# Local attention keys cut into chunks of 96, 96 and 64, twice over

## The chip, the cores and the metric

The kernel runs on one core of a Trainium2 chip. The metric is the device time in microseconds (us). The kernel before takes 934.98 us, the median of three runs (934.98 to 938.12). A core has five engines that work side by side and wait for each other by semaphores: TensorE (PE in the profile; its weight loads are PEld), VectorE (DVE), ScalarE (ACT), GpSimd (POOL) and SyncE (SP), which here only issues DMAs.

## The reference

For 8 batches and 8 heads there are 512 local and 32 global positions of 64 numbers each. A local query attends to the 32 global keys and to the local keys at a distance of at most 32; a global query attends to all 544 keys. The result goes through a feed-forward layer with a softplus in its middle, over 4608 tokens of 512 numbers.

```python
k_all = concat([k_g, k_l]); v_all = concat([v_g, v_l])
out_g = sm(scale * q_g @ k_all.T) @ v_all
s_ll  = where(abs(i - j) <= 32, scale * q_l @ k_l.T, -1e9)
out_l = sm(concat([scale * q_l @ k_g.T, s_ll])) @ concat([v_g, v_l])
x = concat([out_g, out_l]) as [B * S, H * D]
h = x @ w_in                                   # 512 -> 2048
g = maximum(h, 0) + log1p(exp(-abs(h)))
return g @ w_out                               # 2048 -> 512
```

`sm` subtracts the row's maximum, takes exp and divides by the sum plus 1e-9.

## The kernel before

**Tiles.** Two heads make a pair, so there are 32 pairs, four to a batch. The first four pairs (batch 0) go through a scheme of their own in the opening. Each of the other 28 has its local keys cut into six chunks of up to 96, and each chunk stands behind the 32 global keys on the 128 output rows of a score product. The queries are the columns. The 1024 score columns of a head go to two PSUM banks of 512, p = 0 and p = 1. A table `PARTS` says which query columns meet which chunk: 160, 192, 160 columns in the first bank and 32, 192, 192, 96 in the second, that is 7 products a head, 14 a pair (the two heads of a pair work on the two halves of the array's rows). The value products turn chunks back into queries: 8 a head, 16 a pair.

**Softmax without a product.** The maximum over keys of a query lies on partitions, so a transposing reduce (L384, L446) gives maxima or sums of 32 by 32 blocks into a small tile (`mt` for maxima, `zt` for sums), `spread` (L395, POOL) lays its four parts side by side, `gather` (L397 to L405, five small `tensor_reduce` on DVE) folds the blocks that belong to one query or to the global queries, `maxima` copies the answer to the four quadrants of partitions (L410), `lift` (L417) transposes it into a tile of columns that `probs` subtracts on POOL (L429, L431), and `exps` (L435) runs on ACT. For the sums `sums_rest` runs `gather`, four reciprocals (L458) and a transpose (L460). `values_out` multiplies two PSUM banks by that on DVE (L482, 384 and 224 columns), and POOL adds up the global part (L484).

**Feed-forward.** `split_x` (L566 to L579) cuts the attention's result x into a rounded part `xh` (L578, ACT) and the rest `xl` (L579; DVE for the third and fourth pair of a batch, POOL for the others). For every 128 of the 2048 inner features TensorE computes h from xh and xl (12 products of 512 columns), then ACT, DVE (L659) and POOL make `gh` and `gl`, and TensorE computes o from these (12 products).

**Order.** Two lists of step codes set the order of the work on every engine: `OPENING`, and `STEADY`, which runs six times (blocks 1 to 6, four pairs each). S is scores, M maxima, P probs, E exps, Z sums_first, R sums_rest, V values, X and x are split_x of a pair, and h, g, o are a feature block's first half, second half and output. `inorder` chains each engine's instructions in that order. A block ends with "... o R2 E31 h Z3 g X0 X1 R3 o o o V2" and the next starts with "x2 x3 o h g h g": V2 computes the values of two pairs, x2 and x3 split them, and the h that follows opens the next batch. Two shorter lists, `LAST` and `GLOBAL`, close the kernel with feed-forward work alone. PSUM is full: the two `h` banks are shared by the feed-forward's h, by half of a pair's scores and by one of the two value tiles of V2, so the h that follows V2 needs the DVE multiplications that empty that value tile.

**Loads.** For each pair SP loads raw queries and keys (`load`, 736 and 704 columns) and the value chunks.

Of the kernel before, what the change touches and what calls it, by code (L numbers as in the profile page):

```python
# [8 lines left out]
F32 = mybir.dt.float32  # L9
# [12 lines left out]
LOW = -3.0e38  # L22
KW = 96
NPC = 2
QW = (352, 320)
RW = (736, 704)
EW = (0, 736)
FIRST = (0, 9)
PARTS = (((0, 0, 0, 160), (1, 64, 160, 192), (2, 192, 352, 160)),
         ((2, 64, 0, 32), (3, 0, 32, 192), (4, 128, 224, 192), (5, 224, 416, 96)))  # L30
# [33 lines left out]
GW = 76  # L64
# [19 lines left out]
def moe_over_global_local_attention(  # L84
# [57 lines left out]
    def key_masks():  # L142
        near = mask[:, 1]
        nc.vector.memset(near, 0.0)
        for o, w, x0, rows in ((224, 160, 0, P), (32, 64, 0, P), (128, 96, 64, P), (416, 64, 0, 64)):
            r = near[0:rows, o:o + w]
            pool0(nc.gpsimd.affine_select(r, r, pattern=[[1, w]], compare_op=ALU.is_ge, fill=NEG, base=32 + x0, channel_multiplier=-1))
            pool0(nc.gpsimd.affine_select(r, r, pattern=[[-1, w]], compare_op=ALU.is_ge, fill=NEG, base=32 - x0, channel_multiplier=1))
        nc.vector.memset(near[0:32], 0.0)
        for o in (0, 32, 96, 192, 224, 352, 384, 416):  # L150
            nc.vector.memset(near[0:32, o:o + 32], NEG)
        nc.vector.memset(near[64:128, 416:512], NEG)
        for o, w, at in ((256, 160, 0), (32, 192, 160), (224, 160, 352)):
            nc.vector.tensor_copy(mask[:, 0, at:at + w], near[:, o:o + w])
# [167 lines left out]
    def load(m, p):  # L322
        raw = pl.tile([P, rows_of(736)], F32, tag="raw", name=f"raw{m}_{p}", bufs=3)
        order["load"] = after(nc.sync.dma_start(out=raw[:, :RW[p]], in_=qk[m - M0, :, EW[p]:EW[p] + RW[p]]), "load").ins
        st["raw", m, p] = raw
# [6 lines left out]
    def scores(m, p, onv):  # L332
# [26 lines left out]
        inorder(nc.vector.tensor_reduce(windows(mt, 4 + 16 * p, 36, 2, 16), s.rearrange("p h (b k) -> p h b k", k=32),  # L359
# [3 lines left out]
    def scores_all(m):  # L363
# [33 lines left out]
    def gather(mt, op):  # L397
        e0 = 4 * GW + 1
        for u, off in ((-1, 2), (2, 3)):
            inorder(nc.vector.tensor_reduce(grid(mt, e0 + u, (7, 6), (1, 2)), grid(mt, 4 + u - 2 * (u < 0), (12, 6), (1, 2), (off, 2), (GW, 4)), axis=AX.XY, op=op))  # L400
        inorder(nc.vector.tensor_reduce(grid(mt, e0 + 1, (7, 6), (4, 2)), grid(mt, 4 + 1, (12, 6), (7, 2), (GW, 4)), axis=AX.X, op=op))
        g = e0 + 42
        inorder(nc.vector.tensor_reduce(grid(mt, g, (1, 2)), grid(mt, 4 + 4, (36, 2), (12, 3), (3, 2), (GW, 4)), axis=AX.XYZ, op=op))
        inorder(nc.vector.tensor_reduce(grid(mt, e0 + 4, (21, 2), (7, 3)), mt[0:32, g:g + 2].unsqueeze(2).unsqueeze(3).to_broadcast([32, 2, 3, 1]), axis=AX.X, op=op))
        return mt[:, e0:e0 + 42]  # L405

    def maxima(m):
        e = gather(st.pop(("mt", m)), ALU.max)
        for a in range(1, 4):
            inorder(nc.vector.tensor_reduce(e[32 * a:32 * a + 32, 0:40], e[0:32, 0:40].unsqueeze(2), axis=AX.X, op=ALU.max))  # L410
        st["e", m] = e

    def lift(m, p):
        e = st["e", m]
        k = QW[p] // 32
        mb = st["mb", m, p] = pl.tile([P, 2, 352], F32, tag="mb", name=f"mb{m}_{p}", bufs=2)
        inorder(nc.vector.transpose(mb[:, :, :QW[p]].rearrange("p h (s k) -> p h s k", k=32),  # L417
                            windows(e, FIRST[p], 21, 2, k).unsqueeze(3).to_broadcast([P, 2, k, 32])))

    def probs(m, p, engine):  # L420
# [6 lines left out]
        for so, sd, mo, md, w in (((0, 352, 0, 192, 160),), ((32, 192, 0, 128, 192),))[p]:  # L427
            sw = pairs(s, 512, so, sd, w)
            inorder(engine.tensor_tensor(sw, sw, pairs(mb, 352, mo, md, w), op=ALU.subtract))  # L429
        for so, mo, w in (((160, 64, 192),), ((0, 64, 32), (416, 224, 96)))[p]:  # L430
            inorder(engine.tensor_tensor(s[:, :, so:so + w], s[:, :, so:so + w], mb[:, :, mo:mo + w], op=ALU.subtract))  # L431
# [7 lines left out]
    SEG = ((lambda t: t[:, 0:128].unsqueeze(1), 0, 1, 128), (lambda t: windows(t, 160, 224, 2, 192), 128, 2, 192))  # L439

    def sums_first(m):
        zt = pl.tile([P, rows_of(349 + 40)], F32, tag="mt", name=f"zt{m}", bufs=3)
        inorder(nc.gpsimd.memset(zt[0:32, 349:389], 1e-9))
        inorder(nc.gpsimd.memset(windows(zt, 0, 36, 3, 4), 0.0))
        for p in range(NPC):
            inorder(nc.vector.tensor_reduce(windows(zt, 4 + 16 * p, 36, 2, 16), st["s", m, p].rearrange("p h (b k) -> p h b k", k=32),  # L446
# [4 lines left out]
    def sums_rest(m):  # L451
        z0 = gather(st["zt", m], ALU.add)[0:32, 0:40]
        z = st.pop(("zt", m))[:, 0:40]
        inorder(nc.vector.tensor_reduce(z[0:32], bass.AP(z0.tensor, z0.offset, [list(z0.ap[0]), [1, 40], [44, 2]]), axis=AX.X, op=ALU.add))
        zr = pl.tile([P, ROW], F32, tag="zr", name=f"zr{m}", bufs=2)
        for a in range(4):
            h = a // 2
            inorder(nc.vector.reciprocal(zr[32 * a:32 * a + 32, 0:19], z[0:32, 21 * h:21 * h + 19]))  # L458
        rb = st["rb", m] = pl.tile([P, rows_of(608)], F32, tag="rb", name=f"rb{m}", bufs=2)[:, 0:608]
        inorder(nc.vector.transpose(rb.rearrange("p (s k) -> p s k", k=32), zr[:, 0:19].unsqueeze(2).to_broadcast([P, 19, 32])))  # L460

    def values(m, ps):
# [12 lines left out]
    def values_out(m):
# [4 lines left out]
        y = xa[b, j] = pl.tile([P, 608], F32, tag="xa", name=f"xa{b}_{j}", bufs=4)  # L480
# [83 lines left out]
    def split_x(b, j):  # L564
# [263 lines left out]
```

## Time and profile before

| what | value |
|---|---|
| median of 3 runs | 934.98 us (934.98 to 938.12) |
| the profiled execution | 936.42 us, of which span 934.6 us |
| mean granted TensorE clock | 0.998 |
| PE busy | 920.9 us, 99% |
| PE weight loads | 761.8 us, 82% |
| DVE busy | 578.8 us, 62% |
| ACT busy | 496.3 us, 53% |
| POOL busy | 445.8 us, 48% |
| instructions | 14703 |

The span reaches from the first to the last instruction on the core; the execution's own time has about 1.8 us around it. PE's busy time is drawn with modelled ends, so the starts of neighbouring PE rows tell more than their durations. A row such as "x4" is a run of like instructions, and its second column is the time from the first one's start to the last one's end. In brackets stands how long the engine was idle before and what ended the idle time.

### The profile page before, as it was taken

How to read it: one execution, taken by the hardware profiler on the slowest of the kernel's cores; microseconds unless marked ns; L12 is line 12 of the kernel's file. 1: busy time of each engine (PE TensorE's matmuls, PEld its weight loads, DVE VectorE, ACT ScalarE, POOL GpSimd, SP SyncE). 2: the span in 40 equal slices, each digit the busy share in tenths (PEclk: the TensorE clock that was granted, in tenths of full speed). 3: DMA queues.
4: the chain of work that ended last, by engine and by line, in shares of the span. 5: the costliest groups of instructions: out<-in, count | busy, mean ns of one | idle time of the engine just before them, and what ended most of it. 6: DMA issues, size and time to landing. Idle time of an engine off the chain costs nothing.

```text
span 934.6 us, 14703 instructions
## 1 busy us (share of the span) xinstructions
PE 920.9 (99%) x5472; PEld 761.8 (82%) x5472; DVE 578.8 (62%) x1173; ACT 496.3 (53%) x834; POOL 445.8 (48%) x666
## 2 busy tenths in 40 slices
PE   8899999999999999999999999999999999999997
PEld 5778788888888888888888888888888888888896
DVE  5789987576665766567666766567666766311211
ACT  5767777554464535453564636463564626544453
POOL 3344668454554635463654545363644545322221
PEclk9999999999999999999999999999999999999999
DMA  9535431302022030302022030302022020200000
GB/s 354 201 130 192 140 117 64 105 23 77 23 75 67 4 95 5 129 16 83 17 74 72 1 100 1 128 17 83 16 74 70 1 67 1 69 1 1 24 23 23
DMA packets 30696, 64.59 MB, mean 69 GB/s; under 512 B 7328, under 2 KB 7840, under 8 KB 30624
## 3 DMA queue, kind: packets, MB, share of 16 engines
q1 hardware_dynamic: 29888, 63.32, 20.3%
q8 instruction: 43, 0.70, 0.3%
q10 hardware_dynamic: 736, 0.33, 0.2%
q14 instruction: 29, 0.24, 0.1%
HBM read 54.20 MB, written 9.44 MB: 68 GB/s over the span
## 4 chain that ended last, share of the span: by engine, by line
PE 95%; DVE 2%; ACT 2%; issue 0%; ACTq 0%
PE o L157 41%; PE h L157 39%; PE s_ps L157 7%; PE v_ps L157 6%; ACT e L210 1%; PE s L157 1%; PE t L157 1%; DVE sums L207 0%; PE t0g L157 0%; PE dummy L157 0%; PE o0g L157 0%; PE s0g L157 0%; DVE p_1gl L258 0%; DVE wbitswo L610 0%; DVE mb L417 0%
## 5 line engine op out<-in xcount | busy, mean ns | idle before, releaser
L157 PE MATMUL o<-wo,gh 128*128 128x512 f32 x1088 | 340.5, 394 | 0.0
L157 PE MATMUL h<-xh,wi 128*128 128x512 f32 (+1 forms) x1152 | 339.5, 378 | 0.8 <-ACT yg L317 0.8
L663 POOL TENSOR_TENSOR gl<-e,gh 128x512 fp32r<-128x512 f32 x136 | 175.4, 1290 | 310.6 <-ACT gh L662 194.7
L659 DVE SCALAR_TENSOR_TENSOR e<-h,e 128x512 f32<-128x512 f32 x136 | 93.3, 686 | 249.7 <-ACT e L658 242.9
L157 PEld LDWEIGHTS h<-xh,wi 128*128 128x128 f32 x1152 | 212.1, 188 | 41.9 <-ACT yg L317 1.0
L157 PEld LDWEIGHTS o<-wo,gh 128*128 128x128 f32 x1088 | 200.6, 188 | 43.8 <-DVE wo L617 0.2
L157 PE MATMUL h<-xl,wi 128*128 128x512 f32 (+1 forms) x576 | 217.5, 378 | 0.0
L157 PE MATMUL o<-wo,gl 128*128 128x512 f32 x544 | 211.8, 389 | 0.0
L656 ACT ACTIVATE e<-h 128x512 f32<-128x512 f32 x136 | 81.1, 596 | 213.8 <-PE h L157 205.0
L662 ACT CAST gh<-e 128x512 fp32r<-128x512 f32 x136 | 84.4, 621 | 128.5 <-DVE e L659 128.5
L157 PEld LDWEIGHTS h<-xl,wi 128*128 128x128 f32 x576 | 108.4, 188 | 20.8 <-DVE xl L579 0.5
L157 PEld LDWEIGHTS o<-wo,gl 128*128 128x128 f32 x544 | 102.1, 188 | 21.8
L429 POOL TENSOR_TENSOR s<-s,mb 128x640 f32<-128x640 f32 (+1 forms) x55 | 93.9, 1708 | 16.1 <-DVE mb L417 9.6
L658 ACT ACTIVATE e<-e,one 128x512 f32<-128x512 f32 x136 | 98.5, 724 | 4.4
L657 ACT ACTIVATE e<-e 128x512 f32<-128x512 f32 x136 | 86.0, 632 | 4.3
L446 DVE TRANSPOSE_TENSOR_REDUCE zt<-s 128x32 f32<-128x1024 f32 x56 | 67.2, 1222 | 14.9 <-ACT s L435 14.9
L435 ACT ACTIVATE s<-s 128x1024 f32<-128x1024 f32 x56 | 58.5, 1056 | 30.0 <-POOL mt L377 17.0
L157 PE MATMUL s_ps<-raw 64*128 64x192 f32 (+2 forms) x672 | 61.9, 318 | 0.0
L395 POOL COPY mt<-mt 32x76 f32<-32x76 f32 x84 | 20.1, 239 | 83.5 <-DVE mt L384 72.2
L157 PEld LDWEIGHTS s_ps<-raw 64*128 64x128 f32 x672 | 51.9, 187 | 9.8 <-issue 9.6
L384 DVE TRANSPOSE_TENSOR_REDUCE mt<-s 128x32 f32<-128x1024 f32 x48 | 56.6, 1218 | 0.0
L157 PEld LDWEIGHTS v_ps<-s,v 128*64 128x64 f32 x896 | 49.0, 137 | 7.7 <-issue 4.9
(156 smaller groups left out, 845.0 us busy)
## 6 DMA issues: line engine op xcount, KB each, us to landing
raw<-in_qk SPq DMA_DIRECT2D x32, 352.0 KB, 3.0
v<-in_v SPq DMA_DIRECT2D x28, 384.0 KB, 3.3
raw<-in_qk SPq DMA_DIRECT2D x28, 368.0 KB, 3.9
wiraw<-in_w_in SPq DMA_DIRECT2D x16, 512.0 KB, 8.3
woraw<-in_w_out SPq DMA_DIRECT2D x16, 512.0 KB, 6.4
out<-ot SPq DMA_DIRECT2D x32, 256.0 KB, 2.1
v<-in_v SPq DMA_DIRECT2D x4, 512.0 KB, 9.0
raw<-in_qk SPq DMA_DIRECT2D x4, 416.0 KB, 8.6
```

Source lines behind the costliest of these rows:

```text
L157: order["pe"] = after(nc.tensor.matmul(*a, **k), "pe").ins
L384: inorder(nc.vector.tensor_reduce(windows(mt, 4 + 16 * p, 36, 2, 16), st["s", m, p].rearrange("p h (b k) -> p h b k", k=32), axis=AX.X, op ...
L395: inorder(nc.gpsimd.tensor_copy(mt[0:32, GW * a:GW * a + GW], mt[32 * a:32 * a + 32, 0:GW]))
L429: inorder(engine.tensor_tensor(sw, sw, pairs(mb, 352, mo, md, w), op=ALU.subtract))
L435: inorder(nc.scalar.activation(s, s, AF.Exp, scale=0.125))
L446: inorder(nc.vector.tensor_reduce(windows(zt, 4 + 16 * p, 36, 2, 16), st["s", m, p].rearrange("p h (b k) -> p h b k", k=32), axis=AX.X, op ...
L656: inorder(nc.scalar.activation(e, ph, AF.Abs))
L657: inorder(nc.scalar.activation(e, e, AF.Exp, scale=-1.0))
L658: inorder(nc.scalar.activation(e, e, AF.Ln, bias=one))
L659: inorder(nc.vector.scalar_tensor_tensor(e, ph, 0.0, e, op0=ALU.max, op1=ALU.add))
L662: inorder(nc.scalar.copy(gh, e))
L663: inorder(nc.gpsimd.tensor_tensor(gl, e, gh.bitcast(F32), op=ALU.subtract))
```

## The change

A head's local keys are cut into chunks of 96, 96, 64, 64, 96 and 96 (`KEYS`), and its queries start at column 0 and at 224 (`QUERIES`). Both banks then have the same parts, 160, 192 and 160 columns against three chunks of their own, and the same 1024 columns as before: 6 score products a head instead of 7 (12 a pair), 7 value products instead of 8 (14 a pair). What follows from it:

- `gather` has eight `tensor_reduce` instead of five, since the blocks of a query lie in other places; the small tiles have no guard columns any more, so POOL's memsets of them (L350, L377, L444) go. Maxima, sums and reciprocals have 44, 44 and 22 columns for 40, 40 and 19.
- `lift` makes 704 columns for both banks (704 and 640 before), the transpose of the reciprocals 704 for 608.
- `probs` of the second bank is two subtractions for three.
- `values_out` multiplies 352 and 288 columns. POOL's two additions are one of 2 x 32 columns and one of 32.
- `split_x` reads pieces of 2 x 128 and 2 x 160 columns, which overlap (576 columns for 512), where it read 128 and 2 x 192. Both ACT copies come first and then both subtractions; before it was copy, subtraction, copy, subtraction.
- The second load of a pair has 736 columns for 704, and `key_masks` builds the masks with 2 POOL selects for 8 and more DVE copies and memsets.

```diff
-PARTS = (((0, 0, 0, 160), (1, 64, 160, 192), (2, 192, 352, 160)),
-         ((2, 64, 0, 32), (3, 0, 32, 192), (4, 128, 224, 192), (5, 224, 416, 96)))
+KEYS = ((0, 96), (96, 96), (192, 64), (256, 64), (320, 96), (416, 96))
+QUERIES = (0, 224)
+PARTS = ((0, 0, 160), (64, 160, 192), (192, 352, 160))
...
     def gather(mt, op):
-        e0 = 4 * GW + 1
-        for u, off in ((-1, 2), (2, 3)):
-            inorder(nc.vector.tensor_reduce(grid(mt, e0 + u, (7, 6), (1, 2)), grid(mt, 4 + u - 2 * (u < 0), (12, 6), (1, 2), (off, 2), (GW, 4)), axis=AX.XY, op=op))
-        inorder(nc.vector.tensor_reduce(grid(mt, e0 + 1, (7, 6), (4, 2)), grid(mt, 4 + 1, (12, 6), (7, 2), (GW, 4)), axis=AX.X, op=op))
-        g = e0 + 42
-        inorder(nc.vector.tensor_reduce(grid(mt, g, (1, 2)), grid(mt, 4 + 4, (36, 2), (12, 3), (3, 2), (GW, 4)), axis=AX.XYZ, op=op))
-        inorder(nc.vector.tensor_reduce(grid(mt, e0 + 4, (21, 2), (7, 3)), mt[0:32, g:g + 2].unsqueeze(2).unsqueeze(3).to_broadcast([32, 2, 3, 1]), axis=AX.X, op=op))
-        return mt[:, e0:e0 + 42]
+        e0 = 4 * GW
+
+        def fold(out, src, axis):
+            inorder(nc.vector.tensor_reduce(grid(mt, e0 + out[0], *out[1:]), grid(mt, *src), axis=axis, op=op))
+
+        fold((0, (11, 4), (5, 2), (1, 2)), (0, (16, 4), (8, 2), (1, 2), (GW, 4)), AX.X)
+        fold((8, (11, 4), (1, 3)), (13, (16, 4), (1, 3), (GW, 4)), AX.X)
+        fold((2, (11, 4), (1, 3)), (2, (16, 4), (1, 3), (3, 2), (GW, 4)), AX.XY)
+        fold((6, (11, 4), (1, 2)), (9, (16, 4), (1, 2), (2, 2), (GW, 4)), AX.XY)
+        fold((8, (NE, 2), (1, 2)), (13, (32, 2), (1, 2), (3, 2), (GW, 4)), AX.XY)
+        fold((11, (NE, 2), (1, 2)), (e0 + 8, (NE, 2), (1, 2), (1, 1)), AX.X)
+        fold((2 * NE, (1, 2)), (e0 + 4, (NE, 2), (11, 2), (6, 2)), AX.XY)
+        g = e0 + 2 * NE
+        inorder(nc.vector.tensor_reduce(grid(mt, e0 + 4, (NE, 2), (11, 2), (6, 2)), mt[0:32, g:g + 2].unsqueeze(2).unsqueeze(3).unsqueeze(4).to_broadcast([32, 2, 2, 2, 1]), axis=AX.X, op=op))
+        return mt[:, e0:e0 + 2 * NE]
...
-        parts = ((0, 0, 0, 160, 0, 0), (1, 0, 160, 192, 0, 64), (2, 0, 352, 160, 0, 192), (2, 1, 0, 32, 0, 352), (3, 1, 32, 96, 0, 288),
-                 (3, 1, 128, 96, 1, 0), (4, 1, 224, 192, 1, 32), (5, 1, 416, 96, 1, 128))
+        parts = ((0, 0, 0, 160, 0, 0), (1, 0, 160, 192, 0, 64), (2, 0, 352, 160, 0, 192), (3, 1, 0, 64, 0, 256),
+                 (3, 1, 64, 96, 1, 64), (4, 1, 160, 192, 1, 64), (5, 1, 352, 160, 1, 192))
...
-        for bank, at, w in ((0, 0, 384), (1, 384, 224)):
-            inorder(nc.vector.tensor_tensor(y[:, at:at + w], ps[bank][:, 0:w], rb[:, at:at + w], op=ALU.mult))
-        for o in (352, 576):
-            inorder(nc.gpsimd.tensor_tensor(y[:, 128:160], y[:, 128:160], y[:, o:o + SG], op=ALU.add))
+        inorder(nc.vector.tensor_tensor(y[:, 0:QW], ps[0][:, 0:QW], rb[:, 0:QW], op=ALU.mult))
+        inorder(nc.vector.tensor_tensor(y[:, QW:XW], ps[1][:, 64:QW], rb[:, QW + 64:2 * QW], op=ALU.mult))
+        for at, o in ((windows(y, 128, 288, 2, SG), windows(y, 320, 288, 2, SG)), (y[:, 128:160], y[:, 416:448])):
+            inorder(nc.gpsimd.tensor_tensor(at, at, o, op=ALU.add))
...
-    SEG = ((lambda t: t[:, 0:128].unsqueeze(1), 0, 1, 128), (lambda t: windows(t, 160, 224, 2, 192), 128, 2, 192))
+    SEG = ((0, 288, 0, 2, 128), (160, 288, 128, 2, 160))
...
-        for f, o, n, w in seg:
-            hi, lo = (x[j][:, o:o + n * w].rearrange("p (n w) -> p n w", n=n) for x in (xh, xl))
-            onv = j >= 2 if b < B else j % 2
-            inorder((nc.vector.tensor_copy if onv and b == B else nc.scalar.copy)(hi, f(t)))
-            inorder((nc.vector if onv else nc.gpsimd).tensor_tensor(lo, f(t), hi.bitcast(F32), op=ALU.subtract))
+        def parts_of(at, ts, o, n, w):
+            return windows(t, at, ts, n, w), *(windows(x[j], o, 224, n, w) for x in (xh, xl))
+
+        for f, hi, lo in (parts_of(*s) for s in seg):
+            inorder((nc.vector.tensor_copy if onv and b == B else nc.scalar.copy)(hi, f))
+        for f, hi, lo in (parts_of(*s) for s in seg):
+            inorder((nc.vector if onv else nc.gpsimd).tensor_tensor(lo, f, hi.bitcast(F32), op=ALU.subtract))
```

On PE, at the scores of a steady block's third pair, before (`s_ps_0` is the first bank of both heads, `s_ps_10` and `s_ps_11` are the second bank of either head, `raw_0` and `raw_1` the loads of queries and keys):

```order
L157 MATMUL s_ps_0_2514<-raw_0_2424 128x160 x2
L157 MATMUL s_ps_0_2514<-raw_0_2424 128x192 x2
L157 MATMUL s_ps_0_2514<-raw_0_2424 128x160 x2
L157 MATMUL s_ps_10_2515<-raw_1_2426,raw_0_2424 128x32
L157 MATMUL s_ps_11_2516<-raw_1_2426,raw_0_2424 128x32
L157 MATMUL s_ps_10_2515<-raw_1_2426 128x192
L157 MATMUL s_ps_11_2516<-raw_1_2426 128x192
L157 MATMUL s_ps_10_2515<-raw_1_2426 128x192
L157 MATMUL s_ps_11_2516<-raw_1_2426 128x192
L157 MATMUL s_ps_10_2515<-raw_1_2426 128x96
L157 MATMUL s_ps_11_2516<-raw_1_2426 128x96
```

And now, at the same place:

```order
L165 MATMUL s_ps_0_2492<-raw_0_2400 128x160 x2
L165 MATMUL s_ps_0_2492<-raw_0_2400 128x192 x2
L165 MATMUL s_ps_0_2492<-raw_0_2400 128x160 x2
L165 MATMUL s_ps_10_2493<-raw_1_2402 128x160
L165 MATMUL s_ps_11_2494<-raw_1_2402 128x160
L165 MATMUL s_ps_10_2493<-raw_1_2402 128x192
L165 MATMUL s_ps_11_2494<-raw_1_2402 128x192
L165 MATMUL s_ps_10_2493<-raw_1_2402 128x160
L165 MATMUL s_ps_11_2494<-raw_1_2402 128x160
```

The products of 32 columns are gone, and the second bank has the widths of the first.

On DVE, at the end of a steady block (steps R3 and V2, then x2 and x3 of the next block), before (`zt` the sums, `zr` the reciprocals, `rb` their transpose, `v_ps` the values in PSUM, `xa` the attention's result):

```order
L400 TENSOR_REDUCE zt_6609<-zt_6609 32x6x2 x2
L401 TENSOR_REDUCE zt_6609<-zt_6609 32x6x2
L403 TENSOR_REDUCE zt_6609<-zt_6609 32x2
L404 TENSOR_REDUCE zt_6609<-zt_6609 32x6
L454 TENSOR_REDUCE zt_6609<-zt_6609 32x40
L458 RECIPROCAL zr_6650<-zt_6609 32x19 x4
L460 STREAM_TRANSPOSE rb_6655<-zr_6650 128x608
L482 TENSOR_TENSOR xa_2_6710<-v_ps_0_6692,rb_6599 128x384
L482 TENSOR_TENSOR xa_2_6710<-v_ps_1_6693,rb_6599 128x224
L482 TENSOR_TENSOR xa_3_6716<-v_ps_6675,rb_6655 128x384
L482 TENSOR_TENSOR xa_3_6716<-v_ps_6675,rb_6655 128x224
L579 TENSOR_TENSOR xl_2_6727<-xa_2_6710,xh_2_6726 128x128
```

And now, in the same stretch:

```order
L405 TENSOR_REDUCE zt_6572<-zt_6572 32x4x2x2
L405 TENSOR_REDUCE zt_6572<-zt_6572 32x4x3 x2
L405 TENSOR_REDUCE zt_6572<-zt_6572 32x4x2
L405 TENSOR_REDUCE zt_6572<-zt_6572 32x2x2 x2
L405 TENSOR_REDUCE zt_6572<-zt_6572 32x2
L415 TENSOR_REDUCE zt_6572<-zt_6572 32x4x2
L461 TENSOR_REDUCE zt_6572<-zt_6572 32x44
L465 RECIPROCAL zr_6615<-zt_6572 32x22 x4
L467 STREAM_TRANSPOSE rb_6620<-zr_6615 128x704
L486 TENSOR_TENSOR xa_2_6671<-v_ps_0_6655,rb_6562 128x352
L487 TENSOR_TENSOR xa_2_6671<-v_ps_1_6656,rb_6562 128x288
L588 TENSOR_TENSOR xl_2_6688<-xa_2_6671,xh_2_6687 128x2x128
```

The sequence of steps is the same; three more small reduces stand ahead of the reciprocals, and rows of the multiplications that change nothing for what follows are left out at the second listing's end.

## Rows read from the trace of the kernel before

**Rows 1.** The page: busy us of the engines (share of the span, number of instructions), and the shares of the engines in the chain that ended last.

```profile
PE 920.9 (99%) x5472; PEld 761.8 (82%) x5472; DVE 578.8 (62%) x1173; ACT 496.3 (53%) x834; POOL 445.8 (48%) x666
...
PE 95%; DVE 2%; ACT 2%; issue 0%; ACTq 0%
```

**Rows 2.** The chain of waits that ended last, from 538 to 746.6 us (two steady blocks): its shares, then pieces of it in order of time (start, length, engine, what).

```profile
by line: PE o L157 43.0%; PE h L157 41.8%; PE s_ps L157 8.2%; PE v_ps L157 7.1%
...
686.14 3.76 PE v_ps L157 x64
...
705.12 2.14 PE s_ps L157 x28
```

**Rows 3.** PE in order of time at one pair's scores; each row was asked for by itself, from the start that stands first to the end of what the short window took in. Each fp32 product is two passes, and two rows of a kind start for the two heads.

```profile
183.39 0.20 PE L157 MATMUL s_ps<-raw,raw 64*128 64x32 f32 x2
183.42 0.28 PE L157 MATMUL s_ps<-raw,raw 64*128 64x32 f32 x2
183.53 0.41 PE L157 MATMUL s_ps<-raw 64*128 64x192 f32 x2
183.78 0.49 PE L157 MATMUL s_ps<-raw 64*128 64x192 f32 x4
183.94 0.49 PE L157 MATMUL s_ps<-raw 64*128 64x192 f32 x4
...
184.56 0.50 PE L157 MATMUL o<-wo,gh 128*128 128x512 f32 x1
```

**Rows 4.** PE in order of time at one pair's values, asked for in the same way.

```profile
224.81 0.42 PE L157 MATMUL v_ps<-s,v 128*64 128x32 f32 x6
224.87 0.36 PE L157 MATMUL v_ps<-s,v 128*64 128x96 f32 x4
224.98 0.42 PE L157 MATMUL v_ps<-s,v 128*64 128x96 f32 x6
225.06 0.50 PE L157 MATMUL v_ps<-s,v 128*64 128x96 f32 x6
```

**Rows 5.** DVE in order of time around the end of a steady block (start, from first start to last end, idle before).

```profile
680.13 0.69 DVE L659 SCALAR_TENSOR_TENSOR e<-h,e 128x512 f32<-128x512 f32 x1 [1.72 <-ACT e L658]
680.74 0.54 DVE L400 TENSOR_REDUCE zt<-zt 32x12 f32<-32x96 f32 x2
...
683.94 2.33 DVE L446 TRANSPOSE_TENSOR_REDUCE zt<-s 128x32 f32<-128x1024 f32 x2
...
687.23 0.54 DVE L400 TENSOR_REDUCE zt<-zt 32x12 f32<-32x96 f32 x2 [0.39 <-POOL zt L395]
687.70 0.22 DVE L401 TENSOR_REDUCE zt<-zt 32x12 f32<-32x48 f32 x1
687.85 0.22 DVE L403 TENSOR_REDUCE zt<-zt 32x2 f32<-32x48 f32 x1
688.10 0.15 DVE L404 TENSOR_REDUCE zt<-zt 32x6 f32<-32x6 f32 x1
688.29 0.23 DVE L454 TENSOR_REDUCE zt<-zt 32x40 f32<-32x80 f32 x1
...
691.93 1.54 DVE L579 TENSOR_TENSOR xl<-xa,xh 128x128 fp32r<-128x128 f32 x4
```

**Rows 6.** The same place by itself: the first multiplication on DVE, then PE's first h products of the next batch, in order of time.

```profile
690.43 0.52 DVE L482 TENSOR_TENSOR xa<-v_ps,rb 128x384 f32<-128x384 f32 x1
...
691.34 0.63 PE L157 MATMUL h<-xh,wi 128*128 128x512 f32 x2
...
693.17 0.39 PE L157 MATMUL h<-xl,wi 128*128 128x512 f32 x1
...
693.86 0.39 PE L157 MATMUL h<-xl,wi 128*128 128x512 f32 x1
```

**Rows 7.** The groups of DVE instructions over the span, each shape apart (busy us, mean ns of one, idle before).

```profile
L482 DVE TENSOR_TENSOR xa<-v_ps,rb 128x384 f32<-128x384 f32 x28 | 15.2, 543 | 10.7 <-PE v_ps L157 10.6
L417 DVE STREAM_TRANSPOSE mb<-mt 128x704 f32<-128x704 f32 x28 | 25.5, 911 | 1.0
L460 DVE STREAM_TRANSPOSE rb<-zr 128x608 f32<-128x608 f32 x28 | 22.7, 811 | 1.0
L417 DVE STREAM_TRANSPOSE mb<-mt 128x640 f32<-128x640 f32 x28 | 22.4, 802 | 0.0
L482 DVE TENSOR_TENSOR xa<-v_ps,rb 128x224 f32<-128x224 f32 x28 | 10.6, 380 | 0.6
L579 DVE TENSOR_TENSOR xl<-xa,xh 128x384 fp32r<-128x384 f32 x14 | 8.1, 577 | 0.0
L579 DVE TENSOR_TENSOR xl<-xa,xh 128x128 fp32r<-128x128 f32 x14 | 4.4, 312 | 0.0
```

**Rows 8.** ACT's rounding of a pair's x, two single rows of the same boundary.

```profile
691.28 0.51 ACT L578 CAST xh<-xa 128x384 fp32r<-128x384 f32 x1
...
691.74 0.30 ACT L578 CAST xh<-xa 128x128 fp32r<-128x128 f32 x1
```

**Rows 9.** Single rows of PE and DVE in the opening, where PE waits or nearly waits.

```profile
65.59 1.13 PE L157 MATMUL t0g<-diag,e_g 128*128 128x128 f32 x8 [0.61 <-DVE wiraw L611]
...
139.27 0.65 DVE L617 TENSOR_TENSOR wo<-woraw,wo 128x512 fp32r<-128x512 f32 x1
...
139.78 0.69 PE L157 MATMUL o<-wo,gh 128*128 128x512 f32 x2
```

More of the change, by code (lines that the diff above doesn't have):

```diff
@@ L63 @@
 )
-GW = 76
+GW = 64
+NE = 22
 W_PRE = 9
@@ L142, in key_masks @@
     def key_masks():
[L143 to L154, printed above, removed]
+        strip = mask[:, 1, 352:512]
+        nc.vector.memset(mask, 0.0)
+        pool0(nc.gpsimd.affine_select(strip, strip, pattern=[[1, 160]], compare_op=ALU.is_ge, fill=NEG, base=32, channel_multiplier=-1))
+        pool0(nc.gpsimd.affine_select(strip, strip, pattern=[[-1, 160]], compare_op=ALU.is_ge, fill=NEG, base=32, channel_multiplier=1))
+        nc.vector.tensor_copy(mask[:, 0, 0:128], strip[:, 32:160])
+        nc.vector.tensor_copy(mask[:, 0, 352:480], strip[:, 0:128])
+        nc.vector.tensor_copy(mask[:, 1, 0:128], strip[:, 0:128])
+        for p in range(NPC):
+            nc.vector.tensor_copy(mask[:, p, 160:224], strip[:, 0:64])
+            nc.vector.tensor_copy(mask[:, p, 256:352], strip[:, 64:160])
+        nc.vector.memset(mask[:, 1, 480:512], 0.0)
+        nc.vector.memset(mask[0:32], 0.0)
+        for o, w in ((160, 96), (352, 64), (480, 32)):
+            nc.vector.memset(mask[0:32, :, o:o + w], NEG)
+        nc.vector.memset(mask[0:32, 1, 0:64], NEG)
+        nc.vector.memset(mask[0:32, 1, 128:160], NEG)
+        nc.vector.memset(mask[96:128, 0, 352:512], NEG)
+        nc.vector.memset(mask[96:128, 1, 0:160], NEG)
     def mm(*a, **k):
@@ L322, in load @@
     def load(m, p):
-        raw = pl.tile([P, rows_of(736)], F32, tag="raw", name=f"raw{m}_{p}", bufs=3)
-        order["load"] = after(nc.sync.dma_start(out=raw[:, :RW[p]], in_=qk[m - M0, :, EW[p]:EW[p] + RW[p]]), "load").ins
+        raw = pl.tile([P, rows_of(RW)], F32, tag="raw", name=f"raw{m}_{p}", bufs=3)
+        order["load"] = after(nc.sync.dma_start(out=raw[:, :RW], in_=qk[m - M0, :, RW * p:RW * p + RW]), "load").ins
         st["raw", m, p] = raw
@@ L425, in pairs @@
             return bass.AP(base.tensor, base.offset, [list(base.ap[0]), [width, 2], [step, 2], [1, w]])
[L427 to L431, printed above, removed]
+        sw = pairs(s, 512, 0, 352, 160)
+        inorder(engine.tensor_tensor(sw, sw, pairs(mb, QW, 0, 192, 160), op=ALU.subtract))
+        inorder(engine.tensor_tensor(s[:, :, 160:352], s[:, :, 160:352], mb[:, :, 64:256], op=ALU.subtract))
     def exps(m, p):
@@ L464, in values @@
         vt = st.pop(("v", m))
-        parts = ((0, 0, 0, 160, 0, 0), (1, 0, 160, 192, 0, 64), (2, 0, 352, 160, 0, 192), (2, 1, 0, 32, 0, 352), (3, 1, 32, 96, 0, 288),
-                 (3, 1, 128, 96, 1, 0), (4, 1, 224, 192, 1, 32), (5, 1, 416, 96, 1, 128))
-        seen = set()
-        for c, p, o, w, bank, at in parts:
+        parts = ((0, 0, 0, 160, 0, 0), (1, 0, 160, 192, 0, 64), (2, 0, 352, 160, 0, 192), (3, 1, 0, 64, 0, 256),
+                 (3, 1, 64, 96, 1, 64), (4, 1, 160, 192, 1, 64), (5, 1, 352, 160, 1, 192))
+        for i, (c, p, o, w, bank, at) in enumerate(parts):
             for h in range(2):
                 mm(ps[bank][64 * h:64 * h + 64, at:at + w], lhsT=vt[:, h, c], rhs=st["s", m, p][:, h, o:o + w],
-                   start=(bank, h) not in seen, stop=(c, bank) in ((3, 0), (5, 1)), skip_group_check=True)
-                seen.add((bank, h))
+                   start=i in (0, 4), stop=i in (3, 6), skip_group_check=True)
         st["vps", m] = ps
@@ L785, in _layout @@
     v = np.zeros((n, P, 6, D), v_l.dtype)
-    for c in range(6):
-        m = min(KW, SL - KW * c)
+    for c, (k, w) in enumerate(KEYS):
         v[:, 0:SG, c] = vg
-        v[:, SG:SG + m, c] = vl[:, KW * c:KW * c + m]
+        v[:, SG:SG + w, c] = vl[:, k:k + w]
     v = v.reshape(n // 2, 2, P, 6 * D).transpose(0, 2, 1, 3).reshape(n // 2, P, 12 * D)
```

77 lines of the change are left out of this document (36 added, 41 removed).

## The prediction

> **What bounds the kernel now.** I read four views, in this order. The page first: TensorE is busy 920.9 of 934.6 us and holds 95% of the chain that ended last; VectorE, ScalarE and GpSimd are at 62, 53 and 48% [rows 1]. So the question of every edit is what it does to TensorE: its own work, or a wait it has not had. The chain over two steady blocks says the same more sharply: it is TensorE alone, feed-forward o 43.0% and h 41.8%, scores 8.2, values 7.1 [rows 2]. The reader is to see that no wait for another engine is in it at all. Third, TensorE's own rows at one pair's scores and values, asked for start by start, which tell what a product costs beside its columns [rows 3, 4]. Fourth, DVE at the end of a block, where the next batch's h needs what DVE has just written [rows 5, 6]: the one place of each block where TensorE is nearly late.
>
> **What TensorE saves.** The columns stay at 1024 a bank pair, so by columns alone the change saves nothing. But fewer products means fewer short passes. An fp32 product runs in two passes, the two heads side by side. Between two of the 192-column passes lie 0.16 us (183.78 to 183.94), that is 1200 columns a us, so 32 columns should take 0.03. They do take 0.03 from the first pass to the second (183.39 to 183.42), but then 0.11 until the next product starts (183.53), and that one's first pass takes 0.25 instead of 0.16 [rows 3]. Together 0.08 and 0.09 lie over the columns: 0.17 us a pair. My reading is that the weights of the next 128-column product cannot be brought in behind so short a pass. From above: the whole second bank took 1.17 us (183.39 to the o at 184.56) where its 1024 column passes make 0.85, so at most 0.32 is to be had. I take 0.195, near the extra that the rows show, since the 96-column end of the bank leaves only a little more.
>
> The Trainium skill's page "TensorE: Matmul & The Clock Gate", section "Back-to-back issue gap", speaks against this: a product with 1 to 64 columns costs about 60 cycles, a floor of about 25 ns, so by it (my estimate) a 32-column pass costs no more than its columns and taking it out saves nothing. The 0.11 behind the short pass disagrees [rows 3]; the same page's section "LDWEIGHTS", about 1/1.2 ns for each column of weights, estimates 107 ns for 128, which agrees with it.
>
> In the values a 32-column product is followed after 0.06 (224.81 to 224.87) where 0.03 would do, and the next 96-column pass takes 0.11 (to 224.98) where the one after it takes 0.08 (to 225.06) [rows 4]: 0.06 over the columns. The new 64-column product takes 0.055 by its columns, about the weight load it has to cover, so I take 0.055 saved, from 0.03 to 0.06.
>
> 24 pairs run in the steady blocks: 24 x (0.195 + 0.055) = 6.0 us. In the opening the same products save about 2.25 x 0.195 + 4 x 0.055 = 0.67 (fewer of its scores lie on the path, since two banks there are masked by a product of their own; from 0.3 to 1.3). TensorE's side: -6.7 us, from -5.1 to -10.4 (24 x 0.20 and 24 x 0.38 with the opening's ends).
>
> **What DVE gets.** `gather` today is five reduces, 1.06 us from start to start of the next step (687.23 to 688.29). Two that don't need each other start closer than they last (0.15 apart at 687.70, for 0.22), one that needs the one before starts a little later than it ends (0.25 at 687.85, for 0.22) [rows 5]. The eight new ones read 64, 48, 96, 64, 32, 8, 8 and 8 elements a partition; between the rows' 0.15 (6 elements), 0.22 (48) and 0.30 (96, there half of a run of two) that is about 0.25, 0.22, 0.30, 0.25, 0.19 and three of 0.15: 1.67 us, 0.47 more than the five last now. With the first five overlapping as today I get 1.45 from start to start: +0.38. Bounds: +0.28 if the dependent ones cost no gap either, +0.74 if none overlaps. The sums, four reciprocals and the transpose of 704 columns instead of 608 (0.91 for 0.81 [rows 7]) add 0.11, so step R grows by 0.49; step M by 0.51 (its second lift makes 704 columns for 640, 0.91 for 0.80 [rows 7]). All this lies beside TensorE's work unless DVE is late somewhere. POOL loses memsets and one subtraction, hidden by its idle half (48% busy [rows 1]): 0, and a gain if POOL were late somewhere. The loads grow by 32 columns in one of two, about 2% of what a pair loads, a whole block ahead of use, and no DMA stands in the chain [rows 1]: 0, and if a load were late, some 2% of its landing time.
>
> **Where DVE is late.** From 680.13 DVE is busy without a break until the split of x ends, save 0.39 for POOL's spread (687.23); only its first instruction there waited for ACT [rows 5]. In that stretch stand two R steps, R2 and R3, so the first multiplication at 690.43 starts 2 x 0.49 = 0.97 later (the narrower spread gives 0.03 back). It lasts 0.51 (352 columns, by 0.38 for 224 and 0.54 for 384 [rows 7]) and so ends at 691.91. The h product of the next batch, which takes its PSUM bank, started at 691.34, 0.39 after the end of that multiplication (690.95) [rows 6]; with the shorter values it could now start at 691.23, but gets its bank at about 691.99. First stall: 0.75.
>
> Second, x's split. Now the order on ACT is rounding, rounding; on DVE both subtractions follow, each reading both roundings because the pieces overlap, and each piece waits for the one before it that writes the same columns. Rounding 2 x 128 and 2 x 160 columns takes 0.40 and 0.46 (by 0.30 for 128 and 0.51 for 384 [rows 8]); they need both multiplications (692.25), so they end at 693.17; the subtractions (0.44 and 0.51 by 0.31 and 0.58 [rows 7]) end at 694.2. TensorE reads this xl 1.83 after its h starts (693.17 for 691.34 [rows 6]), at 693.82 now: 0.36 more. The fourth pair follows on the same engines: rounded at 694.1, subtracted at about 695.2, read 0.69 after the third (693.86): 0.3 more. Behind the waiting roundings on ACT stand only the next o copies, behind the subtractions on DVE the next e, whose h is late anyway. So a boundary costs 0.75 + 0.36 + 0.34 = 1.45 us; from 1.1 (gather +0.28, an eager overlap) to 1.9 (the chain a little longer on ACT).
>
> Five of the boundaries between batches are of this kind: 7.25. At the last boundary DVE also has a copy of o between the multiplications: 1.6. In the opening TensorE already waits 0.61 for DVE at 65.59, behind M4's gather: its +0.5 goes on top. At 139.78 it reads weights that DVE finishes at 139.92 for the second product, hardly a tenth before it is needed, behind another M step: +0.4 [rows 9]. Smaller places of the opening, among them the masks built at its start, I put at 0.3 together (0 to 0.9). Opening 1.2.
>
> **The sum.** On the profiled execution: -6.7 + 7.25 + 1.6 + 1.2 = +3.4 us, 936.4 to 939.8. That execution is 1.4 above the median; on 934.98 the sum gives 938.4.
>
> **Rivals.**
> (a) Slower: reduces don't overlap where each now waits for another. Gather then costs +0.74, each R step 0.85, a boundary 1.45 + 2 x 0.36 = 2.2; with 2.35 at the last and 1.5 in the opening -6.7 + 14.85 = +8.1: 943. It decides from a stall of about 1.7 a boundary (5 x 1.7 + 1.85 + 1.2 - 6.7 = 4.8). For it: more reduces with a predecessor to wait for. Against: four of the eight have none.
> (b) Faster: the boundary's stalls are hidden, by a shorter gather and by roundings that fit into the time when TensorE waits for h anyway. Then -6.7 + 1.0 = -5.7: 929.3. For it: TensorE arrives earlier than DVE only by tenths. Against: 0.39 of slack against 0.97 of work, with no break in DVE's rows [rows 5, 6].
> (c) The change doesn't do what it says, TensorE saves nothing. Then the boundary has its stalls without the saving: 5 x 1.35 + 1.5 + 1.2 = +9.4: 944.4. For it: the columns are the same. Against: the 0.17 over the columns [rows 3]. The Trainium skill's rule on the issue gap, above, is this rival's mechanism.
>
> **How the numbers follow.** Forecast 0.60, own range 934 to 942; (a) 0.13, (b) 0.13, (c) 0.08, others 0.06. A measurement of this kernel can tell about 0.5% (4.7 us) from no change: faster is below 930.3, slower above 939.65. Faster: (b) and little else, 0.14. Slower: (a), (c) and the upper quarter of the forecast's own range, 0.34. Same 0.52. The range 931 to 944 leaves out most of (b), (c) and the others.
>
> **What would show it.** Scores of a pair at 1.94 instead of 2.14 us in the chain and values of two pairs at 3.65 instead of 3.76 [rows 2]; a DVE gather of eight reduces in about 1.45; the first h behind V2 waiting for the multiplication, with stalls of 0.7, 0.35 and 0.3 at h, third xl and fourth xl in blocks 1 to 6; TensorE's busy time down by 6 to 7 us. I would be wrong if TensorE has no stall at the boundaries, or stalls inside the blocks, in the scores or at gl, which I count at nothing.

## The result

The changed kernel takes 941.36 us, the median of five runs (939.49 to 942.66). The kernel before, with more runs by then, takes 936.32 (934.98 to 938.12). The ratio is 1.0054, 95% interval 1.0035 to 1.0074: a little slower, just over the 0.5% that I called the smallest change to be told from none. The forecast was 938.4 within 931 to 944 (+0.36% on the median of before), with its largest chance, 0.52, on no change to be told and 0.34 on slower. The time is in the range and moved the way the forecast said; by its size it belongs to the slower side.

The runs of either kernel differ by the clock that TensorE was granted in the opening, which is told at the end: before takes 935.0 to 935.1 at a mean of 1.0, after 939.49 at its highest, 0.999. So the change itself costs about 4.4 us, and the profiled pair (936.42 at 0.998, 942.66 at 0.995), 6.2 us apart, overstates it.

The page of the changed kernel, where [rows 1] had 99% and 95% for TensorE:

```profile
span 940.9 us, 14307 instructions
...
PE 920.3 (98%) x5246; PEld 750.8 (80%) x5248; DVE 603.3 (64%) x1343; ACT 498.4 (53%) x834; POOL 439.6 (47%) x577
...
PE 90%; DVE 6%; ACT 3%; issue 1%; ACTq 0%; DVEq 0%
```

DVE and ACT have come into the chain that ended last. The chain of waits from 379 to 486 us, one steady block, shows by which lines, and what the scores of a pair (24 rows of passes now) and the values of two pairs last:

```profile
by line: PE o L165 43.4%; PE h L165 39.5%; PE s_ps L165 7.2%; PE v_ps L165 6.8%; DVE xa L486 0.9%; DVE xl L588 0.9%; ACT xh L586 0.8%; DVE xa L487 0.4%; issue 0.2%
...
395.77 1.94 PE s_ps L165 x24
...
436.81 3.65 PE v_ps L165 x56
```

Against [rows 2] the scores of a pair fell from 2.14 to 1.94 us, the values of two pairs from 3.76 to 3.65, and four steps of a batch's boundary stand where TensorE stood alone: the multiplication of the values (L486, L487), the rounding (L586) and the subtraction (L588). This is DVE at the same boundary as [rows 5], four to five us later in this trace:

```profile
684.45 0.69 DVE L667 SCALAR_TENSOR_TENSOR e<-h,e 128x512 f32<-128x512 f32 x1 [1.37 <-POOL zt L399]
685.06 1.19 DVE L405 TENSOR_REDUCE zt<-zt 32x16 f32<-32x64 f32 x7
686.28 0.15 DVE L415 TENSOR_REDUCE zt<-zt 32x8 f32<-32x8 f32 x1
686.47 0.23 DVE L461 TENSOR_REDUCE zt<-zt 32x44 f32<-32x88 f32 x1
...
688.78 2.33 DVE L453 TRANSPOSE_TENSOR_REDUCE zt<-s 128x32 f32<-128x1024 f32 x2
...
692.04 1.18 DVE L405 TENSOR_REDUCE zt<-zt 32x16 f32<-32x64 f32 x7 [0.35 <-POOL zt L399]
...
695.75 0.49 DVE L486 TENSOR_TENSOR xa<-v_ps,rb 128x352 f32<-128x352 f32 x1
...
697.57 1.88 DVE L588 TENSOR_TENSOR xl<-xa,xh 128x256 fp32r<-128x256 f32 x4 [0.17 <-ACT xh L586]
```

Eight reduces take 1.41 us from start to start of the sum behind them (685.06 to 686.47), 0.35 more than the five of before; from e to the first multiplication it is 11.30 us (684.45 to 695.75) where it was 10.30 (680.13 to 690.43 [rows 5, 6]). TensorE at this boundary, in order of time (the first row is the o in front of it):

```profile
695.29 0.39 PE L165 MATMUL o<-wo,gl 128*128 128x512 f32 x1
696.38 0.70 PE L165 MATMUL h<-xh,wi 128*128 128x512 f32 x2 [0.70 <-DVE xa L486]
...
698.58 0.50 PE L165 MATMUL h<-xl,wi 128*128 128x512 f32 x1
...
699.50 0.50 PE L165 MATMUL h<-xl,wi 128*128 128x512 f32 x1
```

The h behind V2 starts 1.09 after the o before it, where two such rows otherwise start 0.23 apart; the third and fourth xl (698.58, 699.50) come late by tenths more.

The table shows where the time went. It compares the starts of the same feed-forward product in both traces, one product after the other (us, after less before); "by the starts" means this comparison below.

| part of the program | forecast | measured |
|---|---|---|
| start to the first h (59.5 before, 61.0 after) | 0 | +1.44 |
| waits at 65.6 and 82.7 in the opening | +0.8 | +0.41 |
| shorter scores and values in the opening | -0.67 | -0.43 |
| second o product at 140.0 | +0.4 | +1.49 |
| first boundary of batches | 0 | +0.28 |
| 24 pairs' scores, 12 x two pairs' values | -6.0 | -6.18 |
| five boundaries | +7.25 | +7.72 |
| last boundary | +1.6 | +1.68 |
| sum at the last boundary | +3.4 | +6.4 |

The steady part came as worked out; the opening did not, above all at two places. The first row holds 1.67 us of a slower clock, told at the end, and 0.2 us that a pair's shorter scores gave back there.

One sign named in the prediction did not come: TensorE's busy time was to fall by 6 to 7 us and fell by 0.6 (920.9 to 920.3). The slower clock added its 1.67, and of the 11.6 us that the table has lost at waits only 6.9 stand as idle time (span less busy time, 13.7 before and 20.6 after); the rest must be drawn as busy, as in the xl rows above that last 0.50 for 0.39. The saving shows in the starts.

### The profile page after: what moved, and what is told of

Read it like the earlier page. It is cut to its first block, busy times and chain, and to the rows that moved or that the text cites. A ratio compares the mean times of both kernels' runs of the same rounds, so it can differ in the third digit from the quotient of the medians.

```text
span 940.9 us, 14307 instructions
## 1 busy us (share of the span) xinstructions
PE 920.3 (98%) x5246; PEld 750.8 (80%) x5248; DVE 603.3 (64%) x1343; ACT 498.4 (53%) x834; POOL 439.6 (47%) x577
## 4 chain that ended last, share of the span: by engine, by line
PE 90%; DVE 6%; ACT 3%; issue 1%; ACTq 0%; DVEq 0%
PE o L165 39%; PE h L165 37%; PE s_ps L165 6%; PE v_ps L165 5%; ACT e L218 1%; PE s L165 1%; PE t L165 1%; DVE xl L588 1%; DVE sums L215 1%; ACT xh L586 1%; DVE mb L427 1%; PE s0g L165 0%; DVE xa L486 0%; DVE s L362 0%; DVE mt L405 0%
## 5 line engine op out<-in xcount | busy, mean ns | idle before, releaser
L438 POOL TENSOR_TENSOR s<-s,mb 128x640 f32<-128x640 f32 x55 | 86.9, 1580 | 25.4 <-DVE mb L427 25.3
L165 PEld LDWEIGHTS s_ps<-raw 64*128 64x128 f32 x672 | 49.6, 186 | 11.1 <-issue 10.5
L165 PE MATMUL s_ps<-raw 64*128 64x160 f32 (+1 forms) x672 | 57.3, 315 | 0.1
L399 POOL COPY mt<-mt 32x64 f32<-32x64 f32 x84 | 19.1, 228 | 78.7 <-DVE mt L388 67.9
L439 POOL TENSOR_TENSOR s<-s,mb 128x384 f32<-128x384 f32 x55 | 55.9, 1016 | 0.0
```

What stands on the lines that cost most here:

```text
L165: order["pe"] = after(nc.tensor.matmul(*a, **k), "pe").ins
L438: inorder(engine.tensor_tensor(sw, sw, pairs(mb, QW, 0, 192, 160), op=ALU.subtract))
L439: inorder(engine.tensor_tensor(s[:, :, 160:352], s[:, :, 160:352], mb[:, :, 64:256], op=ALU.subtract))
```

## The experiments

All of them ran beside the kernel before on the same chip.

**Two reduces more in the kernel before.** Is it the gather that makes the boundary late, apart from everything else the change does?

```diff
-        inorder(nc.vector.tensor_reduce(grid(mt, e0 + 4, (21, 2), (7, 3)), mt[0:32, g:g + 2].unsqueeze(2).unsqueeze(3).to_broadcast([32, 2, 3, 1]), axis=AX.X, op=op))
+        for _ in range(3):
+            inorder(nc.vector.tensor_reduce(grid(mt, e0 + 4, (21, 2), (7, 3)), mt[0:32, g:g + 2].unsqueeze(2).unsqueeze(3).to_broadcast([32, 2, 3, 1]), axis=AX.X, op=op))
```

> The kernel before with the last small reduce of gather done three times (same values, same place): two more of 0.19 us from start to start, +0.37 a gather, which is what the new gather costs (1.41 for 1.06). Theory (the reduces make the boundary late): at each of the six late boundaries two gathers stand in DVE's unbroken stretch, 0.74 later against 0.39 of slack, so the first h behind V2 starts about 0.35 late and 0.1 is lost at the restart, the xl that follow stay covered: +0.45 each, 2.7 in all; in the opening DVE's weight half at 139.3 moves under a POOL subtraction and lasts 1.3 to 1.7 us instead of 0.65, +1.0 to 1.4. Together about +4 us. Rival (the boundary is late by the new split of x alone): no stall at the boundaries, at most +1.5 from the opening.

Measured: 943.67 us, ratio 1.0081 (1.0063 to 1.0100), so slower than the changed kernel. TensorE's waits, summed over the execution (us, times, longest), and the boundary that answers to the one above:

```profile
PE h L157 <- DVE xa L483: 2.0, 6, 0.3
...
PE o L157 <- DVE wo L618: 1.3, 1, 1.3
```

```profile
694.27 0.53 DVE L405 TENSOR_REDUCE zt<-zt 32x6 f32<-32x6 f32 x3
```

```profile
697.64 0.70 PE L157 MATMUL h<-xh,wi 128*128 128x512 f32 x2 [0.34 <-DVE xa L483]
```

There are six waits for the multiplication where before had none. The starts give 0.58 at each boundary, 0.50 at h and 0.08 behind it, against 0.45 expected: with 0.74 more work on DVE the usable slack was 0.24 and not the 0.39 between the multiplication's end and h's start. No xl is late behind it, as expected, but for 0.13 at the last boundary, and the opening's weight half lost its 1.4 too. The rival (no stall) is out: DVE's reduces alone make the boundary late. The whole came to 8.3 us where about 4 was expected. By the starts the six boundaries cost 3.5, the weight half 1.5 with its restart, and smaller places 0.6; the rest goes with the clock in the opening (a mean of 0.996 in all four runs, 1.0 in four of the eight runs of the kernel before beside them).

**The reduces ahead of the chain, in the changed kernel.** If DVE's unbroken stretch is what is late, taking a piece of it to where DVE waits should give all of it back.

```diff
-    "h g E30 P31 E21 h o Z2 o o g o R2 E31 h Z3 g X0 X1 R3 o o o V2 "
+    "h g E21 E30 h o Z2 P31 o o G2 g o R2 E31 h Z3 g X0 X1 R3 o o o V2 "
...
-        if b and kind in "SMPQEZRV":
+        if b and kind in "SMPQEZRVG":
...
+        elif kind == "G":
+            sums_mid(m)
```

`sums_mid` is the gather and the sum, taken out of `sums_rest`, which does the rest.

> The changed kernel with the third pair's gather and sum taken out of R2 into a step of its own ahead of g (where DVE waits 1.37 us for ACT), its exp ahead of the next pair's on ACT and its sums ahead of the fourth pair's subtraction on POOL. Theory (the boundary is late by DVE's unbroken chain): the chain behind e is 1.41 + 0.26 = 1.67 us shorter, more than the 1.57 us that a boundary loses, so stalls of 0 to 0.2 are left at h, third and fourth xl; 8 to 9 us less than the changed kernel, near 932.5. Rival (something else ends last there: the fourth pair's exp on ACT or the spread on POOL): DVE waits for it instead, over half of the 1.57 us stays, 937 to 940.

Measured: 932.99 us, ratio to the kernel before 0.9963 (0.9950 to 0.9977), 8.4 us less than the changed kernel. DVE around the same boundary, and TensorE at it:

```profile
675.89 1.21 DVE L405 TENSOR_REDUCE zt<-zt 32x16 f32<-32x64 f32 x7 [0.93 <-POOL zt L399]
677.13 0.15 DVE L415 TENSOR_REDUCE zt<-zt 32x8 f32<-32x8 f32 x1
677.32 0.23 DVE L461 TENSOR_REDUCE zt<-zt 32x44 f32<-32x88 f32 x1
677.95 0.69 DVE L674 SCALAR_TENSOR_TENSOR e<-h,e 128x512 f32<-128x512 f32 x1 [0.40 <-ACT e L673]
678.56 1.16 DVE L470 RECIPROCAL zr<-zt 32x22 f32<-32x22 f32 x4
...
687.56 0.48 DVE L491 TENSOR_TENSOR xa<-v_ps,rb 128x352 f32<-128x352 f32 x1
```

```profile
688.86 0.39 PE L165 MATMUL o<-wo,gl 128*128 128x512 f32 x1
689.09 0.61 PE L165 MATMUL h<-xh,wi 128*128 128x512 f32 x2
...
690.90 0.39 PE L165 MATMUL h<-xl,wi 128*128 128x512 f32 x1
691.13 0.61 PE L165 MATMUL h<-xh,wi 128*128 128x512 f32 x2
691.58 0.39 PE L165 MATMUL h<-xl,wi 128*128 128x512 f32 x1
```

The gather runs in front of e, which still waits 0.40 for ACT; from e to the multiplication it is 9.61 us, 1.69 less. The h starts 0.23 behind the o, and no xl is late. By the starts every boundary gives back the 1.54 it had cost, the last one 1.8. Nothing else ends last there, so the rival is out.

**The same reordering in the kernel before** (the edit of the run above, and nothing else).

> Control of run 2: the same reordering in the kernel before. Theory (the reordering pays only where DVE's chain is late, and before it was not): TensorE has no stall there to give back, so the same time within 0.1%, at most 0.5 us less from the last boundary, where TensorE waited 0.2 and 0.1. Rival (the reordering is a gain of its own, whatever the chunks): 2 us or more faster than the kernel before.

Measured: 936.57 us beside 936.57 for the kernel before, ratio 0.9997 (0.9983 to 1.0012). By the starts it gives back 0.3 at the last boundary and nothing elsewhere. So the 0.37% by which the run above beats the kernel before is not the reordering's own: it is what TensorE saves, once the boundaries no longer take it back.

**A product of 160 columns as 32 and 128, and one of 192 as 96 and 96**, in the second score bank of the changed kernel; the two belong together.

```diff
-PARTS = ((0, 0, 160), (64, 160, 192), (192, 352, 160))
+PARTS = (((0, 0, 0, 160), (1, 64, 160, 192), (2, 192, 352, 160)),
+         ((0, 0, 0, 32), (0, 32, 32, 128), (1, 64, 160, 192), (2, 192, 352, 160)))
```

```diff
-PARTS = ((0, 0, 160), (64, 160, 192), (192, 352, 160))
+PARTS = (((0, 0, 0, 160), (1, 64, 160, 192), (2, 192, 352, 160)),
+         ((0, 0, 0, 160), (1, 64, 160, 96), (1, 160, 256, 96), (2, 192, 352, 160)))
```

> The changed kernel, the second score bank's first product of 160 columns cut in two, 32 and 128 columns against the same keys: the same columns, one product a head more, with a short pass again. Theory (a pass shorter than the next 128-column weight load shows the rest of it): scores of a pair 0.17 to 0.20 us longer than the changed kernel's. Rival 1 (each product costs a fixed time of its own): the same 0.20. Rival 2 (the page's issue floor of about 25 ns): 0. Apart from run 4 this run cannot tell the theory from rival 1.

> The changed kernel, the second score bank's 192 columns cut in two products of 96 against the same keys. Theory (only what a pass is shorter than the weight load of about 0.11 us shows): the passes of 96 columns take 0.08 by their columns, four of them lack 0.03 each, so scores of a pair get 0.05 to 0.11 longer. Rival 1 (a fixed time for each product, about 0.1 a pass pair and head as the removed product gave back): 0.20 longer, as with 32 columns. Rival 2: 0.

One execution each: 944.86 and 945.49 us, at different clocks in the opening (1.0 and 0.997). The chain of waits over the same block as above tells them apart, the first for 32 and 128, the second for 96 and 96 columns:

```profile
394.92 2.11 PE s_ps L166 x28
```

```profile
396.45 2.06 PE s_ps L166 x28
```

By the starts the first costs 0.175 us a pair and the second 0.121, with the same columns and the same number of products. A fixed time for each product is out, and so is no cost at all. One number fits both: if a pass ahead of new 128-column weights takes at least a time L from its start to the start of the next, two passes of 0.027 lack 2 x (L - 0.027) = 0.175, so L = 0.11; four passes of 0.08 lack 4 x (L - 0.08) = 0.121, so L = 0.11 again. The starts of the second run's passes show it directly: at 186.50, 186.61, 186.72 and 186.83, 0.11 apart where 96 columns take 0.08. That the weight load is what takes this time is the reading that fits; the runs show the spacing. The second was expected at 0.05 to 0.11 and came just over.

**The opening's weight half moved, on top of the reduces ahead.** In the changed kernel TensorE waits 1.28 us for DVE at the second o product (at 140.0 in the kernel before). Here are TensorE, DVE and GpSimd there:

```profile
142.93 0.50 PE L165 MATMUL o<-wo,gh 128*128 128x512 f32 x1 [1.28 <-DVE wo L625]
```

```profile
141.19 1.69 DVE L625 TENSOR_TENSOR wo<-woraw,wo 128x512 fp32r<-128x512 f32 x1
```

```profile
141.02 1.31 POOL L625 TENSOR_TENSOR wi<-wiraw,wi 128x512 fp32r<-128x512 f32 x1 [0.71 <-ACT wi L624]
142.28 2.03 POOL L438 TENSOR_TENSOR s<-s,mb 128x640 f32<-128x640 f32 x1
```

DVE's instruction lasted 0.65 before [rows 9] and lasts 1.69 now; it ends 0.55 after GpSimd's first one does (142.33), and GpSimd's next, which takes 1.57 at other places, takes 2.03. In the kernel before the order of the two was the other: DVE's started first, at 139.27, and GpSimd's, at 139.53, was the longer one, 1.58 for 1.31.

```profile
139.53 1.58 POOL L617 TENSOR_TENSOR wi<-wiraw,wi 128x512 fp32r<-128x512 f32 x1 [0.53 <-ACT wi L616]
```

```diff
-    "B P61 B h N E60 W g o E61 o M7 n W o N B W W o P70 h N o Z6 N "
+    "B P61 B h N E60 W g o E61 o M7 n T7 W o N B W W o P70 h N o Z6 N "
...
-            for k in range(NPC):
+            for k in range(1 if m == MLAST and not b else NPC):
                 lift(m, k)
+        elif kind == "T":
+            lift(m, 1)
```

> Run 2 with one more step moved, in the opening: DVE's multiplication of a half of o's weights goes ahead of the seventh pair's second lift. It then starts near 140.5 instead of 141.4, while GpSimd is between two of its own. Theory (in the changed kernel and in run 2 it lasted 1.66 to 1.69 us instead of 0.65 because GpSimd worked on two operands of its own beside it, and TensorE waited 1.3 for it): it lasts about 0.65 again, the wait at the second o product near 143 goes, about 1.4 us less than run 2, near 931.5. Rival (that multiplication is long for another reason, such as its operands arriving late from ACT): it keeps 1.3 us or more, and the time stays at 933.

Measured: 930.43 us (928.58 to 932.17, six runs), ratio to the kernel before 0.9930 (0.9912 to 0.9948): faster than both kernels.

```profile
140.97 0.65 DVE L634 TENSOR_TENSOR wo<-woraw,wo 128x512 fp32r<-128x512 f32 x1
```

The multiplication is 0.65 again, TensorE's o products follow at 141.84 and 142.52 without a wait, and by the starts 1.5 us come back there. In the changed kernel ACT's part of its operands had been ready at 139.83, so the rival is out. The medians lie 2.6 us below the run with the reduces ahead, where 1.4 was expected: by the starts 1.5 come back here and 0.3 are lost at the first boundary of batches, and the rest goes with the clock (0.993 to 0.995 there, 0.993 to 1.0 here).

**Pieces of x that don't overlap**, in the changed kernel.

```diff
-    SEG = ((0, 288, 0, 2, 128), (160, 288, 128, 2, 160))
+    SEG = ((0, 0, 0, 1, 128), (160, 288, 128, 2, 160), (352, 0, 288, 1, 64))
```

> The changed kernel with x split in three pieces that do not overlap (128, 2 x 160 and 64 columns, 512 in all) instead of 2 x 128 and 2 x 160. Theory (the second and third stall of a boundary come from roundings and subtractions that wait for each other and from the 64 columns done twice): third xl done about 0.3 earlier, fourth too; of the 0.40 and 0.23 us behind the first stall at most 0.1 each is left, a boundary loses about 1.0 instead of 1.57. Rival (they come from the later start alone, or an instruction more costs as much as the overlap): 1.5 or more. The first stall, 0.94 with its restart, stays by both.

One execution: 939.39 us. The first stall stayed at 0.7 in the profile. By the starts a boundary gives back 0.37 (0.19 at the third xl, 0.11 at the fourth and 0.07 behind it), so it loses 1.17 where the changed kernel loses 1.54; about 1.0 was expected. DVE's rows there run on without a gap:

```profile
694.51 1.76 DVE L588 TENSOR_TENSOR xl<-xa,xh 128x128 fp32r<-128x128 f32 x6
```

Six subtractions of 512 columns each pair in 1.76 us, directly behind the multiplications, are done sooner than four of 576 that wait 0.17 for ACT and last 1.88. So over half of the second and third stall (0.62 with their restarts) was the split; some 0.25 is left.

## Why the prediction was right, and where not

**TensorE's saving** was the safest step and came as worked out: 0.199 a pair of scores for 0.195, 0.058 for 0.055 in the values, 6.18 us in the steady blocks for 6.0. Rival (c), no saving, is out, and with it the rule in the Trainium skill's "TensorE: Matmul & The Clock Gate", section "Back-to-back issue gap", as I had read it for 32 columns: the section gives it for products by themselves, and here each pass has a weight load of its own (5472 of each [rows 1]). The same page's section "LDWEIGHTS" gives a formula by which 128 columns of weights take an estimated 107 ns; the two splits give 0.11, which agrees.

**The gather**: +0.38 predicted, +0.35 measured, the overlap of independent reduces included. Rival (a), no overlap, is out.

**The boundary**: 1.45 predicted, 1.54 measured. The parts are off by more than the sum, so its closeness is in part luck. At h 0.75 was predicted, and 0.86 came with 0.08 at the restart behind it; at the third xl 0.36, and 0.27 to 0.29 came with 0.11; at the fourth 0.34, and 0.12 came with 0.11. Two things shifted between them. The slack at h was smaller than the gap between two rows (0.24 for 0.39): even where h waits for nothing but the multiplication, it starts about 0.15 after the end of it (696.24 to 696.38 in the changed kernel, 697.49 to 697.64 with two reduces more), and 0.39 less 0.15 is 0.24; I had allowed 0.08. And each stall costs about 0.1 more behind it, which I did not count. Rival (b), hidden stalls, is out as a forecast, but it is the state that the reordering reached.

**The opening** is where the sum was off most, and this took the time to the slower side, where the larger chance stood on no change. The step "at 139.78 it reads weights that DVE finishes at 139.92 ... behind another M step: +0.4" had the place and the order right and mis-sized the term: 1.49 were lost. I moved DVE's instruction by what M7 grew and kept its duration. But 0.4 us later it started behind a GpSimd instruction on two operands of its own instead of ahead of it, and waited for that to end. The 1.44 us up to the first h are no loss of the change: in that execution TensorE's clock fell, as told below, and that took 1.67. Without it the profiled difference is 4.6 us, or 4.4 by the runs at the highest clock, against 3.4. A smaller miss is the first boundary of batches, put at nothing, which cost 0.28.

What stays open is the remaining 0.25 of the second and third stall, for which no run was made.

## What to carry to other kernels

A product fewer is worth what its passes fall short of the next weight load, so look for passes of less than about 0.11 us ahead of 128-column weights, and count on nothing from the wider ones. Where an edit puts work on an engine off the critical path, follow that engine's unbroken stretch up to the next instruction that the bounding engine waits for: half a microsecond there, twice, ate the whole gain, and moving the same work to where the engine idles gave it back. And when a shift moves a DVE instruction with two SBUF operands against GpSimd's, its duration is not kept: look what GpSimd does at the new time, and which of the two starts first.

## What the runs showed of the hardware

DVE's two-operand multiplication started 0.17 us after GpSimd's and ended 0.55 after that one's end, nearly its own 0.65 from there; GpSimd's first kept its usual 1.31, and its next one was then longer by 0.46. In the kernel before DVE's started first and kept its 0.65, and GpSimd's was longer by 0.27. So in these rows the one that started first was not slowed and the other waited for it; they did not both run slower. The Trainium skill's page "SBUF — State Buffer", section "SBUF: two separate sides", says that the port pair the two engines share is an exclusive lock held for a whole instruction, which agrees.

TensorE's clock fell to its lower level (1.2 of 2.4 GHz) for some microseconds of the opening in the traces of all kernels here but one, the split into 32 and 128 columns (mean clock 1.000). The two rows below show the stretch from 44 to 48 us (length, busy time and count, granted clock, DMA share, GB/s), in the kernel before and in the changed one:

```profile
44.00:48.00 4.00, 4.00 (x28) 1.00 0.00 0
```

```profile
44.00:48.00 4.00, 4.00 (x14) 0.57 0.00 0
```

Ahead of it TensorE had waited 1.67 us in both, with 2.33 of 4 us busy from 40 to 44, and only in the second the clock fell: the products that follow, with the same columns, took 3.87 us (44.21 to 48.08) instead of 2.20 (44.25 to 46.45). Of 17 runs of the kernel before in the last comparison, six had a mean clock of 1.0 and took 935.0 to 935.1 us; eight had 0.996 or less and took 936.4 to 939.2. So the same program moves by up to 0.4% with it, as much as the change here, and a comparison of a few tenths of a per cent wants the clock beside each time.
